# Second layer's transposed token tiles: every second tile of a pair written to the routing products' PSUM bank instead of the shared one

## The chip, the cores and the metric

One core of one Trainium2 chip runs the whole kernel in one launch. The metric is the device time of one execution in microseconds (us). Engines: PE multiplies matrices, VectorE (DVE) and ScalarE (ACT) work elementwise, GpSimd (POOL) issues gathers and scatters by index, SyncE (SP) issues plain and transposing DMAs. PE writes only to PSUM, of which there are eight banks of 128 x 512 fp32; DVE and ACT copy from there.

## The reference: what is computed

Three layers in a row over 2 x 3584 = 7168 tokens of width 192. First a light convolution: seven weights for each token and head, softmaxed, sum the token and the six before it. Then a mixture of eight experts in which each token takes its best two:

```
noisy = x @ w_gate + log1p(exp(x @ w_noise)) * noise
top2  = two largest of noisy; gates = softmax over the two
out   = sum over the two: gate * (relu(x @ w1[e]) @ w2[e])       # 192 -> 1024 -> 192
```

Then a second mixture of eight experts in which each token takes only its best one: `logits = x @ w_gate`, expert = argmax, gate = its softmax probability. That second layer's logits are what the change is about.

## The kernel before: how the work is tiled and ordered

**Tiles and phases.** A tile is 128 tokens. The 56 tiles are split into two groups: group 0 has 36, group 1 has 20. The first expert layer runs in three phases (0, 1 and 2 in the code: two parts of group 0, then group 1), the second layer in two (3: group 0, 4: group 1). A phase's expert work is a list of units of one or two blocks of 128 gathered rows. A unit makes hidden products in PSUM tiles `ph` (four banks), ACT makes `hh` from them, DVE the rest `hl`, and PE sums the second product in `py` (two banks). Every fp32 product is done as three fp16 products of high and low halves.

**Between the layers.** While the units of phase 2 run, the tokens of group 0 are prepared for the second layer; while those of phase 3 run, group 1. For each batch of two or four tiles a thread `combine_lane` loads a token's two expert results from DRAM (`rows<-ybuf`, `yl<-ybuf`), sums them by their gates, splits the sum into fp16 halves (`rows`) and stores it. `turn_thread` takes the batch, in pairs of tiles: for each tile PE multiplies four 128 x 128 pieces of `rows` by an identity (a transpose), into one PSUM bank, and ACT or DVE (whichever the planner holds free first) copies 128 x 512 out into half of `xtg`, a ring of three pairs. `logit_thread` then makes the batch's logits from `xtg` in one more PSUM tile, and DVE scales them into `lg`. In `settle` DVE picks the expert. When all of a group's batches are through, `route` computes where each token goes; only then can the next phase gather its rows.

**The banks.** The transposes, the logits and the column sums of the weights (`weight_lane`, matmuls of `wacc` and `onesf`) all use one PSUM bank called `pm`. In the program a lock, `ps_lock`, goes with it: `small_ps` waits for it, and it is given back as soon as the reading copy has been issued. On the chip the next matmul into `pm` waits for that copy to end. The products of `route` have a bank of their own, `pr`, which only a route uses; the list `routing` is not empty while a route, an expert choice or the scaling after it (`undo`, `gates`) is being issued. With `ph`, `py`, `pm` and `pr` all eight banks are taken.

**The order.** Each engine runs its instructions in the order in which they were issued, and that order is fixed when the program is built. A planner (`Clock`) keeps an estimated time for every engine and every tile. `Feed.pump`, called after each step of a unit (some ten or twenty `ph` matmuls, or twelve `py` matmuls), runs the waiting threads whose next work is ready by the estimate; a PE step is taken only if its operands and its PSUM tile are estimated free by then. If the estimate is wrong on the chip, an engine waits in order. The planner's run up to the first tile of the second layer is not touched by the diff's condition, since `r.m` is 0 there.

The lock and the allocation of the shared bank, before the change:

```
def small_ps():
    while ps_lock:
        yield None
    ps_lock.append(1)
    return psum.tile([P, 512], F32, name="pm")
```

Of the kernel before, what the change touches and what calls it, by code (L numbers as in the profile page):

```python
# [8 lines left out]
F32 = mybir.dt.float32  # L9
# [7 lines left out]
P = 128  # L17
# [255 lines left out]
def moe_kernel(ctx: ExitStack, tc: tile.TileContext, x: bass.AP, wgen: bass.AP,  # L273
# [14 lines left out]
    def held_pool(name, **kw):  # L288
        return Pool(ctx.enter_context(tc.tile_pool(name=name, bufs=1, **kw)), clk, name.startswith("ps"))
# [12 lines left out]
    psum = held_pool("psum", space=bass.MemoryType.PSUM)  # L302
    ctx.enter_context(tc.manual_schedule())
    ps_lock = []
# [7 lines that stand above are left out]
# [342 lines left out]
    def turn_thread():  # L654

        while True:
            if not queue:
                yield None
                continue
            r, ln, rows, t0, n = queue.pop(0)  # L660
            xts = []
            for a in range(0, n, TPN):
                k = min(TPN, n - a)
                while len(turned) >= XR:
                    yield None
                turned.append(1)
                xt = rt.tile([P, 4 * TPN, P], F16, name="xtg", bufs=XR)[:, 0:4 * k]
                if r is rts[0] and t0 == r.starts[-1]:
                    ps = psp.tile([P, 2, 512], F32, name=f"acc{a // TPN % 2}")
                    yield "P", rows, ps  # L670
                    for v in range(k):
                        for c in range(4):
                            PE.matmul(ps[:, v, c * P:(c + 1) * P], rows.bitcast(F16)[:, a + v, c * P:(c + 1) * P],
                                      ident, start=True, stop=True)
                    for v in range(k):
                        to = xt[:, 4 * v:4 * v + 4].rearrange("p c t -> p (c t)")
                        if v:
                            yield "V", ps, (xt,)
                            V.tensor_copy(to, ps[:, v])
                        else:  # L680
                            yield "A", ps, (xt,)
                            A.activation(to, ps[:, v], AF.Copy)
                elif r.m or t0 == r.starts[-1]:
                    for v in range(k):
                        yield "P", rows
                        ps = yield from small_ps()
                        yield "P", rows, ps
                        for c in range(4):
                            PE.matmul(ps[:, c * P:(c + 1) * P], rows.bitcast(F16)[:, a + v, c * P:(c + 1) * P], ident,
                                      start=True, stop=True)  # L690
                        to = xt[:, 4 * v:4 * v + 4].rearrange("p c t -> p (c t)")
                        if clk.free["A"] <= clk.free["V"]:
                            yield "A", ps, (xt,)
                            A.activation(to, ps, AF.Copy)
                        else:
                            yield "V", ps, (xt,)
                            V.tensor_copy(to, ps)
                        ps_lock.clear()
                else:
                    yield "S", rows, xt  # L700
                    SP.dma_start_transpose(xt, rows.bitcast(F16)[:, a:a + k].rearrange("p t c -> p (t c)"))
                xts += [xt[:, 4 * v:4 * v + 4] for v in range(k)]
            pending[ln] = False
            lqueue.append((r, t0, n, xts))
            yield ()
# [39 lines left out]
    for b in range(B):  # L745
        v = wres[:, 4 + 2 * b:6 + 2 * b].rearrange("p a c -> p (a c)").bitcast(F32)
# [667 lines left out]
    queue, lqueue, turned, pending, routing = [], [], [], [False] * 4, []  # L1414
# [30 lines left out]
    feed.add(first_loads(), -9.0)  # L1445
    feed.add(first_soft(), -1.0)
    logit_ths = [feed.add(turn_thread(), LLATE), feed.add(logit_thread(), LLATE)]
    items = [(r, i) for r in rts for i in range(r.n)]
    early = [(r, i) for r, i in items if r is rts[0] or r is rts[1] and i < BPE]
# [305 lines left out]
    for i in range(nu + 1):  # L1755
# [59 lines left out]
        if i + 3 < nu and units[i + 3].e is None and units[i + 3].ph.known:  # L1815
            v = units[i + 3]
# [36 lines left out]
```

## Time and profile before

| | |
|---|---|
| median of 3 runs | 982.63 us (980.37 to 986.98) |
| the profiled execution | 985.76 us, of which 983.9 us from its first to its last instruction |
| PE busy | 901.3 us (92%), 10522 matmuls |
| DVE, ACT, POOL busy | 754.2, 514.0, 429.7 us |
| mean granted clock of PE | 0.964 of full speed |

The busy time of PE is that of overlapping matmuls, so that what PE loses is read from its idle time, from what ended it, and from the granted clock. In the profile all instructions stand on one line (L190, a recording helper), so groups are told apart by the tiles that they write and read.

### The profile page before, as it was taken

What the parts mean: (1) busy time and instruction counts of PE and PEld (TensorE: products, weight loads), DVE (VectorE), ACT (ScalarE), POOL (GpSimd) and SP (SyncE); (2) the same over time, 40 slices, a digit from 0 to 9 for tenths busy, and PEclk for the clock granted to TensorE, in tenths of its full rate; (3) what the DMA queues carried; (4) which work ended last, traced back from release to release, by engine and by line L of the source; (5) the groups of instructions that cost most, each with busy time, mean ns of one, the idle gap of its engine ahead of it and who ended that gap; (6) DMA issues with size and microseconds to landing.
All of it is one profiled execution on the core that took longest, in us unless ns stands there. A gap on an engine that the chain in (4) does not pass through costs nothing. (4 is left out here: it accounts for less than half of the span.)

```text
span 983.9 us, 26950 instructions
## 1 busy us (share of the span) xinstructions
PE 901.3 (92%) x10522; PEld 834.1 (85%) x10522; DVE 754.2 (77%) x1827; ACT 514.0 (52%) x1040; POOL 429.7 (44%) x574
## 2 busy tenths in 40 slices
PE   1897388899999999999999998999989999999996
PEld 0554388899998999999999998989989999999986
DVE  8587887889998999978498787798588886355453
ACT  1334068674533454653487797645766533444332
POOL 4020044565544555543454453343554544564552
PEclk8898599999999999999999999999999999999998
DMA  9256059968542895852478999853677447462692
GB/s 283 70 136 145 1 152 266 253 156 193 149 116 64 182 215 99 232 131 75 108 200 195 264 264 230 200 121 100 168 173 172 114 123 225 88 118 80 200 258 85
DMA packets 206161, 157.56 MB, mean 160 GB/s; under 512 B 134412, under 2 KB 184927, under 8 KB 206028
## 3 DMA queue, kind: packets, MB, share of 16 engines
q1 hardware_dynamic: 187292, 110.93, 46.2%
q0 software_dynamic: 18736, 44.85, 17.9%
q8 instruction: 84, 1.38, 0.6%
q14 instruction: 49, 0.40, 0.2%
HBM read 74.46 MB, written 32.59 MB: 109 GB/s over the span
## 5 line engine op out<-in xcount | busy, mean ns | idle before, releaser
L190 ACT ACTIVATE hh<-ph 128x512 f16<-128x512 f32 x362 | 214.8, 595 | 261.9 <-PE ph L190 254.8
L190 DVE SCALAR_TENSOR_TENSOR hl<-ph,hh 128x512 f16<-128x512 f32 x362 | 245.6, 684 | 108.7 <-ACT hh L190 100.5
L190 PE MATMUL ph<-xt,wres 128*128 128x256 f16 (+1 forms) x3200 | 320.9, 252 | 4.4 <-ACT xt L190 1.4
L190 PEld LDWEIGHTS <-wres 128*128 128x128 f16 x3200 | 261.5, 99 | 24.4 <-issue 3.9
L190 PE MATMUL py<-wres,hh 128*128 128x192 f16 x2048 | 273.1, 247 | 1.0 <-ACT yo L190 0.8
L190 PEld LDWEIGHTS <-hh 128*128 128x128 f16 x2896 | 260.6, 98 | 5.8 <-issue 1.7
L190 POOL DMA_INDIRECT gt<-rows,src x181 | 197.4, 1091 | 139.4 <-issue 119.7
L190 PE MATMUL py<-wres,hl 128*128 128x192 f16 x1024 | 252.5, 247 | 0.0
L190 POOL DMA_INDIRECT ybuf<-yo,dest x120 | 134.0, 1116 | 250.6 <-ACT yo L190 234.0
L190 PEld LDWEIGHTS <-hl 128*128 128x128 f16 x1448 | 141.9, 98 | 0.5 <-DVE hl L190 0.4
L190 PE MATMUL ph<-xt,w 128*128 128x128 f16 (+1 forms) x1600 | 135.4, 238 | 3.7 <-DMA w<-wres 2.0
L190 PEld LDWEIGHTS <-w 128*128 128x128 f16 x1600 | 113.9, 98 | 10.4 <-DVE w L190 2.6
L190 PE MATMUL py<-w,hh 128*128 128x192 f16 x848 | 113.2, 246 | 0.0
L190 POOL DMA_INDIRECT out_dram<-yo,dest x61 | 62.1, 1018 | 113.9 <-ACT yo L190 71.7
L190 PE MATMUL py<-w,hl 128*128 128x192 f16 x424 | 104.3, 246 | 0.2 <-DVE hl L190 0.2
L190 PE MATMUL acc<-prod,identf 128*128 128x384 f32 x168 | 62.1, 528 | 13.1 <-DVE prod L190 10.7
L190 PEld LDWEIGHTS acc<-prod,identf 128*128 128x128 f32 x168 | 33.8, 206 | 35.4 <-DVE prod L190 10.7
L190 DVE COPY w<-wres 128x3072 f16 x53 | 51.2, 967 | 8.2 <-issue 5.2
L190 DVE SCALAR_TENSOR_TENSOR wres<-w,wsc,wres 128x1024 f16<-128x1024 f32 (+1 forms) x32 | 49.6, 1550 | 7.6 <-ACT wres L190 6.9
L190 ACT ACTIVATE yo<-py 128x192 f32<-128x192 f32 x120 | 37.8, 328 | 28.2 <-PE py L190 22.8
L190 ACT ACTIVATE wres<-w,wsc 128x1024 f16<-128x1024 f32 (+1 forms) x32 | 43.5, 1361 | 10.1 <-DVE wsc L190 9.3
L190 ACT ACTIVATE wres<-w 128x1536 f16<-128x1536 f32 x32 | 47.3, 1477 | 1.6 <-DMA w<-in_moe_w_dram 1.6
(216 smaller groups left out, 930.3 us busy)
## 6 DMA issues: line engine op xcount, KB each, us to landing
w<-wres SPq DMA_DIRECT2D x46, 384.0 KB
rows<-rows SPq DMA_DIRECT2D x24, 512.0 KB
w<-in_moe_w_dram SPq DMA_DIRECT2D x14, 768.0 KB
w<-in_moe_w_dram SPq DMA_DIRECT2D x13, 512.0 KB
xs<-in_x_dram SPq DMA_DIRECT2D x6, 960.0 KB
rows<-ybuf SPq DMA_DIRECT2D x10, 384.0 KB
yl<-ybuf SPq DMA_DIRECT2D x10, 384.0 KB
wres<-wbt SPq DMA_DIRECT2D x56, 64.0 KB
```

Of the source, the lines that this page charges most:

```text
L190: return fn(*args, **kw)
```

## The change

In the branch of `turn_thread` that serves the second layer (and the last batch of each later first-layer part), the second tile of a pair takes a tile of the bank `pr` if the layer is the second and `routing` is empty; it then neither waits for nor gives back `ps_lock`. All else is as before: the same four matmuls, the same copy, by the engine that the planner holds free first.

```diff
                     for v in range(k):
                         yield "P", rows
-                        ps = yield from small_ps()
+                        other = v % 2 == 1 and r.m and not routing
+                        ps = psum.tile([P, 512], F32, name="pr", bufs=1) if other else (yield from small_ps())
                         yield "P", rows, ps
...
-                        ps_lock.clear()
+                        if not other:
+                            ps_lock.clear()
```

## Rows read from the trace of the kernel before

**Rows 1.** The page's busy times: us, share of the span, instructions of each engine.
```profile
PE 901.3 (92%) x10522; PEld 834.1 (85%) x10522; DVE 754.2 (77%) x1827; ACT 514.0 (52%) x1040; POOL 429.7 (44%) x574
```

**Rows 2.** Busy time by stretch: length, each engine's us, granted clock, DMA share, GB/s.
```profile
503.00:554.00 51.00, 50.14 (x708) 47.99 (x705) 44.56 (x135) 36.25 (x83) 24.71 (x33) 1.00 0.91 227
...
582.00:640.00 58.00, 54.76 (x687) 52.33 (x685) 41.94 (x113) 43.63 (x84) 22.84 (x35) 0.94 0.95 208
...
717.00:785.00 68.00, 65.02 (x825) 61.21 (x823) 56.70 (x153) 43.51 (x108) 33.44 (x42) 0.97 0.64 153
```

**Rows 3.** Tile `pm`, 500 to 785: operation, count, ns min/median/max, first and last start.
```profile
L190 PE MATMUL pm<-ident,rows x224: 216/219/311, 503.0 to 781.7; 128*128 128x128 f16 x112
L190 PE MATMUL pm<-gwh,xtg x224: 166/166/214, 508.3 to 783.2; 128*128 128x8 f16 x112
...
L190 DVE CAST xtg<-pm x29: 668/691/693, 504.0 to 782.0; 128x512 f16<-128x512 f32 x29
L190 ACT ACTIVATE xtg<-pm x27: 577/597/608, 506.0 to 778.8; 128x512 f16<-128x512 f32 x27
```

**Rows 4.** PE's waits from 500 to 785: us in total, times, longest.
```profile
PE pm L190 <- ACT xtg L190: 4.7, 2, 3.2
PE pm L190 <- DVE xtg L190: 1.4, 3, 0.8
PE ph L190 <- DVE hl L190: 1.4, 1, 1.4
...
PE ph L190 <- DMA gt<-rows,src: 1.0, 1, 1.0
```

**Rows 5.** Instructions in order of time: start, us, what, idle before and releaser.
```profile
596.60 0.39 PE L190 MATMUL pm<-ident,rows 128*128 128x128 f16 x4
...
598.91 0.39 PE L190 MATMUL pm<-ident,rows 128*128 128x128 f16 x4
...
601.97 0.60 ACT L190 ACTIVATE xtg<-pm 128x512 f16<-128x512 f32 x1
...
605.74 0.39 PE L190 MATMUL pm<-ident,rows 128*128 128x128 f16 x4
...
607.15 1.49 ACT L190 ACTIVATE rows<-rows,gate 128x192 f32<-128x192 f32 x4 [3.85 <-DMA rows<-ybuf]
...
610.79 0.58 ACT L190 ACTIVATE xtg<-pm 128x512 f16<-128x512 f32 x1
...
611.42 0.58 PE L190 MATMUL pm<-ident,rows 128*128 128x128 f16 x4 [3.21 <-ACT xtg L190]
```

**Rows 6.** The same view, another batch of group 1.
```profile
727.47 0.38 PE L190 MATMUL pm<-ident,rows 128*128 128x128 f16 x4 [0.22 <-DVE xtg L190]
...
732.86 0.39 PE L190 MATMUL pm<-ident,rows 128*128 128x128 f16 x4
...
734.06 0.59 ACT L190 ACTIVATE xtg<-pm 128x512 f16<-128x512 f32 x1
...
734.70 0.38 PE L190 MATMUL pm<-ident,rows 128*128 128x128 f16 x4 [1.45 <-ACT xtg L190]
...
735.86 0.33 PE L190 MATMUL pm<-ident,rows 128*128 128x128 f16 x3 [0.78 <-DVE xtg L190]
```

**Rows 7.** Two stretches right behind those waits, columns as in Rows 2.
```profile
611.42:617.10 5.68, 5.68 (x61) 5.48 (x61) 3.87 (x10) 4.02 (x9) 3.16 (x5) 0.50 0.85 251
...
736.60:740.00 3.40, 3.40 (x36) 2.57 (x35) 1.29 (x7) 0.87 (x2) 1.73 (x2) 0.51 0.57 133
```

**Rows 8.** Order of time: the two second-layer routes' first products, and the scaling between.
```profile
643.53 0.29 PE L190 MATMUL pr<-msk,ones 128*128 128x288 f16 x1
...
710.84 0.33 DVE L190 TENSOR_REDUCE undo<-rc 128x21 f32<-128x168 f32 x1
...
789.49 0.23 PE L190 MATMUL pr<-msk,ones 128*128 128x160 f16 x1
```

**Rows 9.** Order of time: the only logits for which PE waited.
```profile
524.18 0.17 PE L190 MATMUL pm<-gwh,xtg 128*128 128x8 f16 x1 [0.41 <-DVE xtg L190]
```

## The prediction

> **What bounds the kernel now.** I read the busy times first: PE has 901.3 us of a span of 983.9 [rows 1], so a change pays only where it gives PE time back. Next the stretches in which second-layer tiles are turned. The three in [rows 2] hold 51.00, 58.00 and 68.00 us, of which PE is busy 50.14, 54.76 and 65.02: idle 0.86, 3.24 and 2.98, in all 7.08 us. That is all that better ordering can give directly there; in addition the granted clock is below full in two of them (0.94 and 0.97). Then what passes through the shared bank [rows 3]: 224 transposes, four to a tile, so 56 tiles; 29 copies by DVE at 691 ns and 27 by ACT at 597 ns, which also makes 56. Last, who makes PE wait [rows 4]: copies out of the shared bank five times, 4.7 + 1.4 = 6.1 us. So 51 of the 56 reuses cost PE nothing: the planner puts steps of expert work between one tile's transposes and the next's, and PE does those while the copy runs.
>
> **What the change does, step by step.** Nothing is added or left out: 224 transposes, 56 copies and their logits stay. Of the 56 tiles, 28 are the second of a pair and move to the routing bank. The first of the next pair then waits for the first of this one, and the second for the second: every reuse of a bank has one copy more between it and its predecessor. In the program the second tile of a pair need not wait for an estimated copy any more, so that it can follow the first in one turn of the planner; logits come up to two steps sooner.
>
> *Is the other bank free?* The routes' first products are at 643.53 and 789.49 [rows 8]; the turned tiles' logits run from 508.3 to 783.2 [rows 3], group 0's before the first route and group 1's after it. The scaling that also fills the list of routes is short (its last step is 0.33 us at 710.84 [rows 8]). So nearly all of the 28 tiles should get the bank.
>
> *Direct waits removed.* The worst is at 611.42: that tile is the second of its pair and waits 3.21 us for the copy of the first, which ACT begins only at 610.79, after it has itself waited 3.85 us for loaded results [rows 5]. In group 1, the tile at 734.70 waits 1.45 us for the copy of the tile at 732.86, and the tile at 735.86 another 0.78 us for the next copy; 727.47 has 0.22 us [rows 6]. With two banks each of these finds its own bank free or older by a copy: 3.21 + 1.45 + 0.78 + 0.22 = 5.66 us. The fifth wait, 0.41 us [rows 9], is that of logits for the last copy and does not depend on the bank; it stays.
>
> *Clock.* Behind these waits PE ran at the lower of its levels: granted clock 0.50 for 5.68 us from 611.42, and 0.51 for 3.40 us from 736.60 [rows 7]. At half speed half of the time is lost: 5.68 x 0.50 + 3.40 x 0.49 = 2.84 + 1.67 = 4.51 us. If the idle time ahead of them goes, this goes too. The most that can come back is thus 5.66 + 4.51 = 10.17 us.
>
> *What is late next.* Copies are not made faster. In the batch of [rows 5], the second tile's copy began 601.97 - 598.91 = 3.06 us after its transposes began, the third's 610.79 - 605.74 = 5.05 us, because ACT was behind the planner's estimate. Now fewer places wait for copies (in a batch of four tiles: third tile, fourth tile and logits; before: second, third, fourth and logits), but they stand nearer together and the logits need all four. If the whole batch comes ahead of ACT's 3.85 us wait, the 3.21 us are gone; if it falls behind, the logits wait in the place of the fourth tile. Bounds: nothing back (0) and all (10.17). I take half, 5.1 us, because the waiting places per batch go from four to three while the margin of each in the estimate is as before, and because two of the four waits are for a second tile's copy or by a second tile whose place in the order moves a whole step.
>
> *Other costs.* Two copies back to back can hold up the next `hh` or `hl` by one copy, 0.60 or 0.69 us [rows 3]; the four `ph` banks cover this, since PE's steps go on, and the one wait for `hl` is 1.4 us [rows 4]. Without that cover it would be 28 times 0.69 = 19 us; below, a gain, I see none, since the copies' number is the same. I take 0, because there is one such wait in 285 us. Transposes into the second bank carry a wait on whichever engine last read it; the shortest such wait that shows is 0.22 us [rows 6], so at most 28 x 0.22 = 6 us, at least 0, and I take 0, because 51 of 56 transposed tiles have a like wait and no idle time. The turning step issues no DMA, but once a batch has been turned, its lane may issue the next loads on SP's queue; the DMA engines' share is 0.91 and 0.95 in group 0's two stretches [rows 2], so they would queue there behind others: 0, with 3.85 us of one such late load [rows 5] as the bound either way. Column sums of weights find the shared lock open sooner; that helps ACT and DVE, not PE: 0. A route that starts sooner can take up the 1.0 us for the first gather of phase 3 [rows 4]: between 0 and 1.0, and I take 0, since POOL issues that gather in order behind scatters of results.
>
> **Sum.** Against the profiled execution: 985.76 - 5.1 = 980.7 us. This execution is 3.1 us above the median of the runs shown, 982.63, and I carry the difference over to the median: 982.6 - 5.1 = **977.5 us**.
>
> **The rivals.** *The wait comes back at the logits, same size.* PE's idle time moves from the fourth tile to the logits. For it: ACT's lag of 3.06 and 5.05 us is not touched. Against: three of the four waits are on the bank alone. Gain 0 to 2: about 982.
>
> *All of it comes back.* Both batches get ahead of ACT's and DVE's lag, full clock returns, and phase 3's first gather is in time: 10.17 + 1.0 = 11.2, so 971.4. Against: the 3.85 us late load is still in ACT's queue, ahead of some copy.
>
> *Every reuse costs a copy.* If each second tile's turn cost PE one copy, 28 x (29 x 0.691 + 27 x 0.597) / 56 = 28 x 0.646 = 18.1 us would come back: 964.5. The rows speak against it: PE has 7.08 us of idle time in all there. The Trainium skill (Perfetto Trace Analysis, section Matmuls) says that independent groups of matmuls should rotate through different banks, so that the copying of one overlaps the next group's matmuls; by that rule taken alone this is the case to expect. The trace agrees only in part: the copy is overlapped already, by other engines' banks and other matmuls, in 51 of 56 cases.
>
> *Slower: logits too near.* Logits now follow the last transposes sooner. There are 16 batches (224 products of the first kind in [rows 3], four a tile, in batches of two or four tiles: four of two, twelve of four). If in each PE waited one DVE copy, 0.69 us, that is 11.0 us, and if the old waits only moved here and none of the 10.17 came back, the time is 982.6 + 11.0 = 993.6. It decides once the logits stand within one step of PE (about 1 us: transposes 0.39 and copy 0.69) behind the fourth tile's transposes. Against: only one logits batch waited, 0.41 us [rows 9], and the planner requires the last copy's estimated end, as before.
>
> *It doesn't do what it says.* If `routing` were held through most of the turning, the order would be nearly the old one: 982.6. The times of [rows 8] speak against it.
>
> **How the numbers follow.** Half comes back 0.40; it comes back at the logits 0.28; all comes back 0.16; logits too near 0.08; does not act 0.04; every reuse costs a copy 0.02; the 0.02 left is a re-planned order that loses elsewhere. One per cent, 9.8 us, is about what a measurement of this kernel can tell from no change (its three runs lie 6.6 us apart). Faster by over 1%, below 972.8: two thirds of "all", the 0.02 of "every reuse", and 0.03 of "half" where late loads shift in its favour: 0.16. Slower, above 992.5: about half of "too near" and half of the rest: 0.05. Same: 0.79. The range goes from 970, which takes in "all" (971.4) with a late load's scatter, to 988, which takes in "comes back" (982) plus the 6 us bound on the new waits; outside are 964.5, 993.6 and some scatter, under 0.2.
>
> **What would show it.** Right: tiles of `pr` written by the transposes 112 times, copies from both banks, PE's waits on the shared bank's copies down from 6.1 to some 3 us, no stretch at clock 0.50 behind 611 or behind 735. The rival at the logits: PE's idle time ahead of the logits products, for a copy, of 2 us or more. Too near: small waits ahead of most of the 16 logits. Doesn't act: no transposes in the routing bank. The forecast is wrong if PE's idle time between 503 and 785 hardly changes, or if the time moves while it does not.

## The result, and the profile after

The change made the kernel slower: a median of 992.89 us (991.56 to 995.54, 4 runs) beside 983.21 us for the kernel before (980.37 to 986.98, 4 runs); the ratio is 1.0102, 95% interval 1.0062 to 1.0142. The forecast was 977.5 in a range of 970 to 988. The profiled execution took 991.89 us, with a span of 990.1; against the profiled execution before (985.76) that is 6.1 us of the medians' 9.7.

First PE's busy time on the page of after, which answers to [rows 1]: the same work, in a longer span.

```profile
PE 901.0 (91%) x10522; PEld 833.7 (84%) x10522; DVE 750.6 (76%) x1823; ACT 513.5 (52%) x1044; POOL 434.1 (44%) x574
```

Then the three stretches of [rows 2], and a fourth row that is explained below (length, busy us of PE, its weight loads, DVE, ACT, POOL, granted clock, DMA share, GB/s):

```profile
503.00:554.00 51.00, 50.37 (x712) 48.46 (x710) 45.28 (x147) 37.59 (x85) 25.74 (x35) 1.00 1.08 242
582.00:640.00 58.00, 48.68 (x603) 45.80 (x601) 38.44 (x102) 38.03 (x76) 23.50 (x32) 0.91 0.85 201
717.00:785.00 68.00, 63.95 (x855) 60.54 (x854) 55.98 (x169) 47.87 (x123) 32.91 (x42) 1.00 0.82 169
603.98:609.10 5.12, 5.12 (x27) 4.05 (x28) 4.51 (x22) 2.95 (x10) 2.00 (x3) 0.50 0.15 22
```

The loss stands in the second row: PE's idle time there is 58.00 - 48.68 = 9.32 us, before it was 3.24. The third has 4.05, before 2.98. What passed through the second bank (operation, count, ns min/median/max):

```profile
L190 PE MATMUL pr<-ident,rows x112: 216/219/220, 503.0 to 777.3; 128*128 128x128 f16 x112
...
L190 DVE CAST xtg<-pr x15: 671/683/692, 505.7 to 777.5; 128x512 f16<-128x512 f32 x15
L190 ACT ACTIVATE xtg<-pr x13: 582/592/606, 504.1 to 776.5; 128x512 f16<-128x512 f32 x13
```

The change did act: 112 transposes, 28 tiles, went to the second bank. PE's waits from 500 to 785, which answer to [rows 4] (us in total, times, longest):

```profile
PE pm L190 <- DVE ss L190: 9.3, 1, 9.3
PE py L190 <- ACT yo L190: 2.7, 3, 1.8
PE ph L190 <- DMA gt<-rows,src: 1.6, 1, 1.6
...
PE pm L190 <- DVE xtg L190: 0.6, 2, 0.4
...
```

The five waits for copies, 6.1 us, have shrunk to two, 0.6 us; so far the forecast held (how much of it is the bank's doing is asked in experiments 2 and 3). In their place stands one wait of 9.3 us. In order of time (start, us, what, idle before and what ended it) it looks like this:

```profile
591.14 0.18 DVE L190 TENSOR_TENSOR lg<-lg,sm 128x32 f32<-128x32 f32 x1
...
591.65 4.92 SPq L190 DMA_TRANSPOSE xt<-gt  x2
...
596.68 0.52 SPq L190 DMA_DIRECT2D w<-in_moe_w_dram  x1
597.24 1.45 SPq L190 DMA_DIRECT2D rows<-gt  x1
598.80 1.92 SPq L190 DMA_TRANSPOSE xt<-gt  x1
...
603.54 0.29 DVE L190 TENSOR_SCALAR lg<-pm,ix,gwt 128x32 f32<-128x32 f32 x1 [12.22 <-issue]
603.56 0.07 DVE L190 MEMSET gt<- 128x16 f32 x1
...
603.98 0.56 PE L190 MATMUL pm<-wacc,onesf 128*128 128x1 f32 x2 [9.32 <-DVE ss L190]
```

DVE does nothing for 12.22 us. In its order of instructions the one after `lg<-lg,sm` is the clearing of `gt` (`V.memset(gt, 0.0)` in `settle`); the `lg<-pm` row only starts 0.02 us sooner in the record (in experiment 1, which has the same order, the three start at 589.27, 589.40 and 589.71). `gt` is a small tile in a ring of four (`bufs=NC2 + 1`): each batch clears one, puts its gates in, and SP stores it to DRAM (`rows<-gt`); the `gt` of gathered rows, in `gt<-rows,src` and `xt<-gt`, is another tile of that name. The seventh batch needs the third batch's buffer, and the third batch's store is the SP row at 597.24. It is the 301st DMA that SP issues in the trace; in the kernel before, the third batch's store was the 285th and went out at 577.54 (the expectation of experiment 6 counts in the program, 46 higher):

```profile
577.54 0.59 SPq L190 DMA_DIRECT2D rows<-gt  x1
```

The sixteen that stand ahead of it in the changed kernel, and behind it before, are the two loads of the next batch (`rows<-ybuf`, `yl<-ybuf`), two stores of `rows`, four transposing DMAs and eight loads of weights. PE, which needs DVE for the next expert work, has no work from 594.67 on. Behind the wait it runs at the lower of its two levels, 0.50 (the fourth row above), for 5.12 us, of which half is lost: 2.6 us.

A second such wait, shorter, is in group 1. DVE again, in order of time:

```profile
758.60 0.18 DVE L190 TENSOR_TENSOR lg<-lg,sm 128x32 f32<-128x32 f32 x1
763.69 0.17 DVE L190 TENSOR_REDUCE ss<-lg 128x4 f32<-128x32 f32 x1 [4.91 <-ACT rows L190]
763.70 0.07 DVE L190 MEMSET gt<- 128x16 f32 x1
```

The record names ACT as the releaser, but the clearing that starts with it waits in the program for the store of group 1's first batch. PE's wait of 1.8 us for `yo` at 771 follows in time; that the one causes the other is not shown.

### The profile page after: what moved, and what is told of

It is laid out like the page before. It is cut to its first block, busy times and chain, and to the rows that moved or that the text cites. A ratio compares the mean times of both kernels' runs of the same rounds, so it can differ in the third digit from the quotient of the medians.

```text
span 990.1 us, 26968 instructions
## 1 busy us (share of the span) xinstructions
PE 901.0 (91%) x10522; PEld 833.7 (84%) x10522; DVE 750.6 (76%) x1823; ACT 513.5 (52%) x1044; POOL 434.1 (44%) x574
## 4 chain that ended last, share of the span: by engine, by line
PE 29%; DVE 7%; issue 6%; DMA 4%; POOL 2%; ACT 1%; SPq 1%; DVEq 0%; POOLq 0%; ACTq 0%
PE ph L190 15%; PE py L190 12%; DVE hl L190 2%; DMA gt<-rows,src 2%; PE pm L190 1%; DMA xt<-gt 1%; POOL out_dram L190 1%; DVE yl L190 1%; POOL gt L190 1%; PE pr L190 1%; DVE w L190 1%; SPq L190 1%; DMA w<-wres 1%; DMA yl<-ybuf 1%; ACT hh L190 0%
## 5 line engine op out<-in xcount | busy, mean ns | idle before, releaser
L190 POOL DMA_INDIRECT gt<-rows,src x181 | 199.4, 1102 | 134.5 <-issue 120.0
L190 POOL DMA_INDIRECT ybuf<-yo,dest x120 | 137.5, 1146 | 253.7 <-ACT yo L190 236.6
```

The lines of the kernel that those rows point to most:

```text
L190: return fn(*args, **kw)
```

## The experiments

The theory: the second bank does what it was meant to, and the loss is DVE's waits for `gt` buffers whose stores stand late in SP's queue. The main rivals: SP and the DMA engines are behind there anyhow, so that another wait would take its place; or the new order loses a little in many places. "Same order" below means that every engine has the same instructions in the same order as in the kernel that the experiment starts from. Experiments 1 to 4, 5 to 8 and 9 to 11 ran on three chips, each group beside the kernel before; a ratio is to that kernel on the same chip.

**1. Six buffers, same order.**

```diff
-gt = pool.tile([P, NJ, RW - 256], F32, name="gt", bufs=NC2 + 1)[:, 0:n]
+gt = pool.tile([P, NJ, RW - 256], F32, name="gt", bufs=NC2 + 3)[:, 0:n]
```

> The changed kernel with six buffers in place of four for the small tile gt that settle clears and stores; the order of every engine's instructions is the changed kernel's. Theory (the loss is one wait: DVE's clearing of a gt buffer waits for the store of an earlier gt, which stands late in SP's queue, and PE behind it idles 9.3 us and then runs at half clock for 5.1 us): that wait goes, PE's idle time before the column sums at about 604 falls from 9.3 us to under 1, and the time falls by 9 to 12 us, to 981 to 984. Rival A (SP's queue and the DMA engines are behind at that point, and the next work that needs them waits instead): 989 or more, with PE idle 5 us or more between 590 and 612. Rival B (the new order loses in many small places, this wait being only the largest): 985 to 988.

Measured: 979.45 us beside 982.30 for the kernel before, ratio 0.9984 (0.9962 to 1.0006): 13.4 us less than the changed kernel's median on its own chip, or 11.6 us by the two ratios, which is within the 9 to 12 expected; the time itself is 1.5 us below the expected band. In order of time, the same clearing (the seventh) and the same store:

```profile
589.40 0.07 DVE L190 MEMSET gt<- 128x16 f32 x1
...
597.11 1.13 SPq L190 DMA_DIRECT2D rows<-gt  x1
```

The store is as late as it was; the clearing just no longer waits for it. PE's waits, 500 to 785:

```profile
PE ph L190 <- DVE hl L190: 2.8, 1, 2.8
PE ph L190 <- DMA gt<-rows,src: 1.7, 1, 1.7
...
```

So rival A is right about 2.8 us (DVE is then held by loaded rows that come late), with 3.41 us at half clock behind them, and wrong about the rest; rival B falls.

**2. Control: six buffers in the kernel before.** The same edit there.

> The kernel before with six gt buffers, same order as before. Theory: no such wait there, since the third batch's store went out at 577; time within 2 us of the kernel before. Rival (four buffers are short for any order, and cost the kernel before too): 980 or less.

Measured: 983.14, ratio 1.0014 (0.9986 to 1.0041). As the theory says: the ring is no limit in the old order. The trace of this control shows one thing more. With one bank and the old order, PE's waits for copies from 500 to 785, and the stretch from 582 to 640, were:

```profile
PE pm L190 <- ACT xtg L190: 1.4, 1, 1.4
...
PE pm L190 <- DVE xtg L190: 1.4, 3, 0.8
...
```
```profile
582.00:640.00 58.00, 58.00 (x754) 55.85 (x752) 46.63 (x125) 48.49 (x94) 28.57 (x40) 1.00 1.04 237
```

The waits of group 1 [rows 6] are there again, 0.22, 1.45 and 0.78 us, with no half clock behind them. The wait of 3.21 us [rows 5] and its half clock are not; ACT had its loaded rows in time. In experiment 4, where group 0 also has the old bank and order, that wait is 2.10 us. So the largest wait that the prediction counted comes and goes between executions without any change of bank.

**3. Two banks on the chip, one in the planner.** `small_ps` gives the second tile of a pair the bank `pr`, keeps the lock, and tells the planner that the tile comes free when the last user of either bank is through.

```diff
...
-        return psum.tile([P, 512], F32, name="pm")
+        t = psum.tile([P, 512], F32, name="pr" if other else "pm")
+        if last_ps:
+            clk.floor[t.tensor.name] = clk.acc.get(last_ps[0], 0.0)
+        last_ps[:] = [t.tensor.name]
+        return t
...
-                        ps = yield from small_ps()
+                        ps = yield from small_ps(v % 2 == 1 and r.m and not routing)
```

> Every second tile of a pair in the second layer uses the routes' bank, as in the change, but the planner is told that both banks are one, so that each engine's instructions stand in the order of the kernel before. Theory (the second bank by itself does what the prediction counted; the loss comes with the new order): PE's waits for copies out of the shared bank fall from 6.1 us to 1 or less, the two stretches at half clock behind them go, and the time is 5 to 10 us below the kernel before: 973 to 978. Rival (the wait only moves to the logits, which stand where they stood and need the same late copies): 981 to 984. Rival (the second bank itself costs something): 986 or more.

Measured: 978.50, ratio 0.9975 (0.9947 to 1.0002): half a microsecond above the expected band. By the medians that is 3.8 us below the kernel before, by the ratio 2.5, and the interval just reaches 1. PE's waits from 500 to 785, and the stretch that held the worst one:

```profile
PE ph L190 <- DMA xt<-gt: 1.6, 2, 0.8
PE ph L190 <- DVE hl L190: 1.4, 1, 1.4
PE pr L190 <- ACT xtg L190: 1.2, 1, 1.2
...
```
```profile
582.00:640.00 58.00, 58.00 (x763) 55.96 (x762) 46.24 (x131) 46.92 (x93) 27.71 (x39) 1.00 1.00 240
```

Copies cost PE 1.2 us, in place of 6.1 in [rows 4] and of 2.8 in experiment 2. The stretch from 582 to 640 has no idle time and full clock, where [rows 2] had 3.24 us and 0.94; but so it has in experiment 2 with one bank, so that this can't be put down to the second. The bank by itself is no loss; whether its gain is 0 or 5 us the interval leaves open.

**4. The change for group 1 alone.**

```diff
-other = v % 2 == 1 and r.m and not routing
+other = v % 2 == 1 and r.m and not routing and r.g == 1
```

> The change for the 20 tiles of group 1 alone; up to group 1's first tile the order is that of the kernel before. Theory (the loss arises in group 0's batches): the 9.3 us wait does not occur, group 1's waits of 2.2 us and its half-clock stretch of 3.4 us go, new waits of some 2 us in group 1 stay: 979 to 984. Rival (the new order loses in group 1 as well): 987 or more.

Measured: 981.93, ratio 1.0011 (0.9983 to 1.0038). Neither loss nor gain. In one point the expectation missed: a stretch of 3.4 us at half clock stays at 732, behind a wait of 1.3 us for a copy by DVE. It is the logits that wait there.

**5. Five buffers.** As experiment 1 with `NC2 + 2`.

> The changed kernel with five gt buffers, order unchanged. Now it is the batch after, one gt later (13 DVE instructions further on), whose clearing waits for the same late store. Theory (what counts is when that store lands, about 603.5 us, not how many buffers there are): DVE is held from about 592 to about 603, PE a little less than with four buffers, 6 to 9 us, half clock behind it; time 988 to 992. Rival (one more buffer is slack enough, the wait is absorbed by the work that stands between): 979 to 983, as with six.

Measured: 984.07 beside 983.97, ratio 1.0014 (0.9987 to 1.0040). Both expectations missed. The wait itself came as the theory said, one batch later; in order of time:

```profile
592.82 0.19 DVE L190 TENSOR_TENSOR lg<-lg,sm 128x32 f32<-128x32 f32 x1
...
597.83 1.75 SPq L190 DMA_DIRECT2D rows<-gt  x1
...
605.50 0.17 DVE L190 TENSOR_REDUCE ss<-lg 128x4 f32<-128x32 f32 x1 [12.50 <-issue]
605.51 0.07 DVE L190 MEMSET gt<- 128x16 f32 x1
...
607.38 1.04 PE L190 MATMUL ph<-xt,wres 128*128 128x256 f16 x4 [8.52 <-DVE hl L190]
```

PE loses 8.52 us there, near the 9.32 of four buffers. What I had left out is the second wait: with five buffers the clearing at 763.70 has no store to wait for, and group 1's stretch is as good as with six (the row from 717 to 785, first with five, then with six):

```profile
717.00:785.00 68.00, 67.10 (x871) 63.43 (x869) 59.79 (x188) 46.82 (x120) 35.75 (x44) 1.00 0.68 157
```
```profile
717.00:785.00 68.00, 67.12 (x834) 63.35 (x832) 60.28 (x187) 43.69 (x109) 33.22 (x43) 1.00 0.63 142
```

So the five-buffer kernel sorts the two waits apart. From the first turned tile to the first transposes of phase 3, and from there to the start of PE's last matmul, the profiled executions took:

| | to phase 3 | from there |
|---|---|---|
| before | 692.75 - 503.05 = 189.7 | 281.4 |
| before, six (experiment 2) | 691.54 - 507.37 = 184.2 | 280.4 |
| two banks, old order (experiment 3) | 689.19 - 504.76 = 184.4 | 279.3 |
| changed, four buffers | 699.53 - 502.81 = 196.7 | 280.8 |
| five | 696.99 - 501.15 = 195.8 | 275.9 |
| six | 689.96 - 500.93 = 189.0 | 276.2 |

The first wait, with its clock, is worth 196.7 - 189.0 = 7.7 us, the second some 4.6 to 4.9 us (in which a half clock of 3.4 us near 701 is contained, which the runs with five and six buffers do not have). Experiments 2 and 3 differ in the bank, and in the ring that is no limit there, and are 0.2 us apart up to phase 3 and about 1 behind it; so in these traces the bank is worth about 1 us. Of the 3.3 us between their profiled executions (983.44 and 980.13), 2.6 lie ahead of the first turned tile (507.37 and 504.76), where the bank is not used yet. The changed order also keeps a loss that six buffers do not cure: 189.0 up to phase 3 beside 184.2, most of it the wait of 2.8 us and the half clock behind it in experiment 1. It makes this good behind phase 3's start (276.2 beside 280.4).

**6. The stores first.** The threads of `settle` are preferred by 3 us in the planner, with four buffers; the stores go out earlier and the order of other work moves with them.

```diff
-feed.add(settle(r, t0, n), C2LATE)
+feed.add(settle(r, t0, n), -3.0)
```

> The changed kernel with four gt buffers as it was, but the settle threads, which issue the small stores, preferred by 3 us in the planner: the third gt store now stands at place 283 of SP's queue, in place of 347, and the order of other things moves with it. Theory (the store's place in SP's queue made the wait): no wait of DVE for a gt buffer over 1 us, PE's waits for copies as low as in the changed kernel, time 977 to 983. Rival (the stores only take the place of loads in SP's queue, so the combining lanes starve): 986 or more, with PE or DVE waiting for loaded rows.

Measured: 977.63 beside 983.97, ratio 0.9940 (0.9914 to 0.9965), faster than the kernel before by more than the noise. The third store leaves at 523.24, and the three after it by 549.33:

```profile
523.24 0.36 SPq L190 DMA_DIRECT2D rows<-gt  x1
...
538.80 0.37 SPq L190 DMA_DIRECT2D rows<-gt  x1
...
544.88 2.10 SPq L190 DMA_DIRECT2D rows<-gt  x1
...
549.33 0.53 SPq L190 DMA_DIRECT2D rows<-gt  x1
```

No clearing waits, and the two stretches that hold nearly all the turning have PE busy 135.30 of 137 and 140.70 of 145 us:

```profile
503.00:640.00 137.00, 135.30 (x1765) 129.44 (x1763) 113.94 (x323) 106.84 (x217) 64.19 (x89) 1.00 1.05 240
640.00:785.00 145.00, 140.70 (x1765) 133.87 (x1763) 118.35 (x331) 90.98 (x198) 67.36 (x90) 0.99 0.60 138
```

Copies cost PE 2.2 us here, not the 0.6 of the changed kernel, so that part of the expectation missed.

**7. The change for group 0 alone.** As experiment 4 with `r.g == 0`.

> The change for the 36 tiles of group 0 alone. Theory: up to 640 us the order is the changed kernel's, so the 9 us wait and the half clock behind it are there: 989 to 995. Rival (the loss needs group 1's new order too): 985 or less.

Measured: 991.37 beside 983.97, ratio 1.0084 (1.0056 to 1.0113), with PE's wait there again:

```profile
PE pm L190 <- DVE ss L190: 9.8, 1, 9.8
```

With experiment 4: the net loss comes with group 0's part of the change.

**8. Control: the stores first in the kernel before.** The edit of experiment 6 there.

> The kernel before, one shared bank, with the settle threads preferred in the planner by 3 us as in the run before last. Theory: nothing waited for a gt buffer there, so that nothing is to be had but what the re-planned order scatters: 978 to 988. Rival (early stores are worth something by themselves, and explain the gain of preferring them in the changed kernel): 977 or less.

Measured: 981.68, ratio 0.9978 (0.9949 to 1.0006). Within what was expected; a small gain from early stores alone is not excluded.

**9 to 11** ran as one group on another chip, on which every kernel, the one before included, took some 6% longer (1041.43 us for the kernel before); only ratios within that group are used. **9** is the changed kernel again, with no edit.

> The changed kernel itself, beside the two others of this group. Theory (two waits of DVE for gt buffers, one of some 12 us in group 0 and one of some 5 us in group 1, are the whole loss): 990 to 995, both waits in its profile at the same instructions. If it came out below 987, the loss would not be a property of the order.

Measured: ratio 1.0038 (1.0002 to 1.0073). The loss is there but smaller than the 1.0102 of the first measurement; 990 to 995 would be 1.007 to 1.012, so the size missed. At 1.0038 the kernel would take 986.9 us on the first chip, just at the 987 below which the expectation would no longer call the loss a property of the order; that the whole 1.0% goes with the order is not borne out on this chip. The first wait is in its profile, the second is not, so that this half of the expectation missed too: no clearing of `gt` in group 1 comes after an idle time of 2 us or more.

```profile
640.71 0.56 PE L190 MATMUL pm<-wacc,onesf 128*128 128x1 f32 x2 [8.71 <-DVE ss L190]
```

**10** is experiment 6 with six buffers (`NC2 + 3`), same order as experiment 6.

> The changed kernel with the settle threads preferred (the order of the run with the stores first) and six gt buffers. Theory: with the stores early no clearing waits, so more buffers add nothing: within 2 us of that run's 977.6. Rival (buffers still short there): 975 or less.

Measured: ratio 0.9958 (0.9924 to 0.9992), beside 0.9940 in experiment 6. The times can't be compared, but the ratios agree: with early stores more buffers add nothing that shows.

**11** is experiment 3 with the edit of experiment 6: two banks in the order of experiment 8.

> Two banks on the chip, but the planner is told they are one, in the order of the kernel before with the settle threads preferred (the order of the run that had 981.7 with one bank). Theory: the second bank takes away PE's waits for copies, 3 us there, and nothing else changes: 976 to 980, 2 to 5 us below that run. Rival (in this order the second bank is worth nothing, since PE waits at the logits): within 1 us of 981.7.

Measured: ratio 0.9936 (0.9896 to 0.9975), beside 0.9978 with one bank in experiment 8. The difference goes the way of the theory, 0.4%, but the intervals overlap; it is not settled.

## Why the prediction was wrong, point by point

*That the other bank is free* was right: all 28 tiles got it. *The direct waits* were right in kind: waits for copies fell from 6.1 to 0.6 us, and 5.5 us is near the 5.66 counted. That nearness is in part luck: with one bank and the old order, experiment 2 had 2.8 us of such waits, without the one of 3.21 us. *The clock*: no half clock remains at 736 [rows 7], and in group 0 it stands behind another wait; but experiment 2 has no half clock in these stretches either. So of the bound of 10.17 us, 3.21 + 2.84 + 1.67 = 7.72 us came from one profiled execution and are no fixed price of the shared bank; the term was mis-sized, and 2.45 us is what both executions have. Half of 10.17 us, 5.1, was the forecast; by the medians, the bank without the new order brought 3.8 (experiment 3), and the change with the ring's wait taken away 2.9 (experiment 1), with intervals that both reach 1. The logits did not become the place of waiting (the longest such wait is 0.40 us, at 528.67), so that neither the rival at the logits nor the slower one came. Nor did every reuse turn out to cost a copy: the 18.1 us of that rival stand against 3.8 us for the bank alone. The rule of the Trainium skill (Perfetto Trace Analysis, section Matmuls) that independent groups rotate through banks held here by that size at most, since only five waits for copies (four in experiment 2) were there to be taken away.

*The step that failed*, and that turned a gain into a loss, is in "Other costs": that once a batch is turned "its lane may issue the next loads on SP's queue", priced at 0 with 3.85 us as the bound. This was the right queue and the wrong victim. I priced the loads themselves and did not ask what else stands in SP's queue that somebody waits for. It is the small store of the gates: sixteen places later, issued at 597.24 in place of 577.54. Who waits for it is not the reader in DRAM but the next clearing of its buffer on DVE, four batches on, in order ahead of all that PE needs from DVE. Its price was 9.32 us of idle time and 2.6 us of clock, more than the whole gain that was in reach. In the kernel before nothing waited there, so no row of the trace could show the ring as short; the ring of four and the store that frees it can be read in `settle` alone, and I had not counted how many stores were still out.

The account of the 7.0 us that the profiled executions lost up to phase 3: 9.32 + 2.6 lost; 3.21 (the copy's wait) + 2.84 (its clock) regained; phase 3's first gather 1.61 + 0.6 in place of 1.02, 1.2 lost; sum 7.1. The 3.21 + 2.84 belong to a wait that experiment 2, with the bank unchanged, does not have; beside that execution the loss up to phase 3 is 196.7 - 184.2 = 12.5 us. After it 0.6 us is gained: 2.45 us of copies' waits and 1.67 us of clock came back, and the second clearing and a half clock of 3.4 us near 701 took nearly as much. The 3.6 us by which the medians differ more than the profiled executions are in no trace.

What stays open: why the planner put the third store so much later. That batches turned sooner let their lanes' loads reach SP first, and that the planner takes a step on SP only when its estimate holds SP free, fits the order and the gain of preferring the stores (experiment 6), but no experiment undid that alone.

## What to carry to other kernels

When a step is sped up whose successors issue DMAs, list every instruction that waits for anything in that queue, also for a buffer to come free, and count how many buffers are out at once in the new order, not only in the old. A wait that took no time in the trace of before is no proof of slack: in the kernel before, the third store left at 577.54 and its buffer was cleared again at 598.50, while the fourth store, for which a ring of three would have waited, left only at 598.49. Nor is a wait in one trace a price yet: a control with the same order, as experiment 2, shows whether it comes again. And test a resource and an order apart: the same bank with the old order, and the same order with a longer ring, told in two runs what the change alone could not.

## What the runs showed of the hardware that was not expected

A store of one batch's gates, 8 KB in 512 pieces of 16 bytes, was issued at 597.24 and let DVE go at 603.54, 6.3 us later, with the DMA engines' share at 1.23 (the packets' times added up, so that it can pass 1) between 594.67 and 603.98:

```profile
594.67:603.98 9.31, 0.00 (x0) 0.03 (x1) 0.40 (x4) 0.00 (x0) 0.00 (x0) 0.73 1.23 225
```

Most of the 6.3 us is not the store itself. In the DMA packets of the trace its 512 pieces move from 602.43 to 602.67, so that 5.2 us pass before the first of them; in experiment 6 the store issued at 523.24 had them moving from 524.13 to 524.49.

And the same change cost 1.0% on one chip and 0.4% on another, on which the kernel before took 6% longer; what made that chip slower was not looked into.
